# Later blocks of a blocked FFT convolution transformed by residue, with half the matrix products and a second butterfly level on VectorE

## The chip, the cores and the metric

The kernel runs on one core of a Trainium2 chip. TensorE (PE) does matrix products into PSUM, VectorE (DVE) and ScalarE (ACT) do elementwise work, GpSimd (POOL) a little of it, and SyncE (SP) issues most transfers. The metric is the device time of one execution in microseconds (us). Three runs of the kernel before gave 387.19, 388.03 and 388.34 us; the median is 388.03.

## The reference

Two layers of the same two sub-blocks over x of 2048 rows by 512 channels, in bf16. Sub-block A is a gated long convolution, sub-block B a SwiGLU feed-forward network (FFN):

```python
def A(q, k, v, shift_k, ssm_k, ssm_D):          # S = 2048, D = 512
    k_shift = sum(k_pad[:, t:t + S] * shift_k[:, ks - 1 - t] for t in range(4))
    kv = k_shift * v
    y = irfft(rfft(kv, 2 * S) * rfft(ssm_k, 2 * S))[:S]      # along the sequence, per channel
    return q * (y + kv * ssm_D)

def B(x):                                        # F = 1792
    return (silu(x @ w_gate) * (x @ w_up)) @ w_down

x = A_q
x = x + A(layernorm(x), A_k, A_v, ...);  x = x + B(layernorm(x))
x = x + A(layernorm(x), A_k, A_v, ...);  x = x + B(layernorm(x))
```

k, v and the filter do not depend on x, so the convolution result y is the same in both layers and is computed once.

## The kernel before

**Convolution.** The sequence is cut into NB = 4 blocks of L = 512 rows; block b of y is a sum of products of spectra of blocks i and j with i + j = b (an odd-frequency transform of length N = 1024). A block's 512 rows are stored as 128 partitions by R = 4 residues. A spectrum is a tile [128, 4, 2, 512]: four slots of 128 frequencies, a real and an imaginary part, 512 channels. A transform is done partly as products with the constant matrices `fwd` (line 264) and partly as sums and differences on VectorE:

- `spectrum_h(b)` (398): `transpose_h` turns the filter block into rows, `half` (328) makes eight PSUM tiles, two accumulated products of 512 columns each, which ScalarE copies out (`evacuate`, 320); `butterfly` (339) is one level of sums and differences, two VectorE operations of 2048 elements; then `G`, a combination of two blocks' spectra.
- `spectrum_x(b)` (412): `shift_mul` (385) makes the shifted k by 64 small products and multiplies it by v on VectorE, straight out of PSUM (395); then `half` and `butterfly`.
- `product(i, j)` (420): the complex product of X[i] and G[j], 2048 elements to an operation, added into Z[i + j].
- `inverse(k)` (474): two 2048-element operations into `su`, then four PSUM tiles of four accumulated products each, copied out by ScalarE as Y[k].

Block 0 has a path of its own (`direct`, `inverse_direct`).

**FFN.** `ffn` (569) handles a unit: one layer, one block, one half (two of the four residues, 256 rows). In groups of up to four of the 14 tiles of F it makes gate and up products (line 590, by the helper on 252), Silu and copy on ScalarE (593, 597), one multiplication on VectorE (600, tile `ht`), and down products (607) into two PSUM tiles `pd`; at the end VectorE adds these to x (612), and in layer 1 the rows are stored. There are 16 units, in the order block, layer, half. `prologue` (536) comes before a unit: layer norm (`ln_stats`, `normalise`; the reciprocal root on GpSimd, 516), the gating with y (543, 544), the second norm and a transposing transfer of z to `zT`.

**Order.** Nothing is issued where it stands in the text. `add` gives each operation to a `Plan` with an engine, an estimated cost, the buffers that it touches and, for some, a due time; `dues` (99) works due times backwards, and `order` (112) then writes each engine's order out: always the operation that can start first, and among those that can start at about the same time the one with the earliest due time. At run time each engine works its list off in that order. Buffers come from rings of fixed size (228): `pf` 4 and `pc` 2 and `pd` 2 PSUM tiles (FFN, convolution, down products), `s8` 10 spectra, `ht` 5. FFN units get due times from T0 on, DC = 22 us to a unit and DF = 18 in the last block (684). Until T0, idle stretches of PE are filled with dummy products (`dummy`, 179).

**Start.** SP issues k, h, v of block 0, then w_gate, x of block 0, w_up, w_down, x of block 1 (the order that the planner made); ScalarE's queue brings the taps (`tapT`) and D (`dcol`). ScalarE makes `fwd` with a Sin (640) and afterwards runs one Silu ahead of time (643).

Of the kernel before, what the change touches and what calls it, by code (L numbers as in the profile page):

```python
# [9 lines left out]
P = 128  # L10
# [8 lines left out]
NB = 4  # L19
SLK = 5.0  # L20
R = 4

# [23 lines left out]
class Plan:  # L46
# [143 lines left out]
def kernel(  # L190
# [36 lines left out]

    plan = Plan({"h": 1, "k": 1, "v": 1, "hs": 1, "x": 2, "y": 2, "s8": 10, "t4": 2, "n": 2, "z": 3, "zT": 3,
                 "sg": 2, "ht": 5, "st": 8, "mv": 6, "ve": 6, "rs": 6, "pf": 4, "pc": 2, "pd": 2})
# [41 lines left out]

    def load_h(b):
        hn[b] = new("h", "hn", [P, KD, L], parts=1)
        add("SP", 0.55, lambda: nc.sync.dma_start(out=hn[b].t[:], in_=h3[:, :, b * L:(b + 1) * L]), w=[hn[b]], lat=4.5)

    def load_k(b):
        kT[b] = new("k", "kTb", [P, KD, PADL + L], parts=2)
        if b == 0:
            add("POOL", 0.2, lambda: nc.gpsimd.memset(kT[b].t[:, :, 0:PADL], 0.0), w=[(kT[b], (0,))])
            add("SP", 1.5, lambda: nc.sync.dma_start_transpose(out=kT[b].t[:, :, PADL:PADL + L], in_=k3[0:L]),  # L280
                w=[(kT[b], (1,))], lat=3.5)
# [4 lines left out]
    def load_v(b, eng="SP"):  # L286
        vt[b] = new("v", "vt", [P, R, D], parts=R)
        q = nc.sync if eng == "SP" else nc.scalar
        add(eng, 0.6, lambda: q.dma_start(out=vt[b].t[:], in_=v_t[:, b]), w=[vt[b]], lat=4.5)

    def load_x(c):
        xs[c] = new("x", "xc", [P, R, D], parts=R)
        add("SP", 0.7, lambda: nc.sync.dma_start(out=xs[c].t[:], in_=q_t[:, c]), w=[xs[c]], lat=4.5)

    def load_weights(which):
# [4 lines left out]
        add("SP", 0.6, lambda: nc.sync.dma_start(out=wt[which].t[:], in_=src), w=[wt[which]], lat=12.0)  # L300

# [83 lines left out]
    def shift_mul(b, ring, conv):  # L385
        for r in range(R):
            ps = new(ring, "ps", [P, D], F32)

            def go(ps=ps, r=r):
                for dt in range(KD):  # L390
                    mm(ps.t[:, dt * P:(dt + 1) * P],
                       [(kT[b].t[:, dt, PADL + r - j:PADL + r - j + R * (P - 1) + 1:R], dg.t[:, dt, j, :])
                        for j in range(KS)])
            add("PE", pe(KS * KD, P), go, r=[kT[b], dg], w=[ps], conv=conv)
            dve(D, lambda ps=ps, r=r: nc.vector.tensor_tensor(out=vt[b].t[:, r, :], in0=ps.t[:], in1=vt[b].t[:, r, :],  # L395
                                                             op=ALU.mult), [ps], [(vt[b], (r,))], one=True, conv=conv)

    def spectrum_h(b, ring="pc"):
# [7 lines left out]
        h, hp = H[b], H[b - 1]  # L406
        for part, op in ((0, ALU.subtract), (1, ALU.add)):
# [4 lines left out]
    def spectrum_x(b):  # L412
        shift_mul(b, "pc", True)
        ev = spectrum("ev")
        X[b] = spectrum(f"X{b}")
        for par in (0, 1):
            half(vt[b], ev, par, 1.0, "pc", ("ACT", "ACT"), True)
        butterfly(ev, X[b], None, True)

# [54 lines left out]
    def inverse(k):  # L474
        y, z = new_y(k), Z[k]
        su = spectrum("su")
        dve(4 * D, lambda: nc.vector.tensor_add(out=su.t[:, 0:2], in0=z.t[:, 0:2], in1=z.t[:, 2:4]), [z],
            [(su, key((0, 1)))], conv=True)
        dve(4 * D, lambda: nc.vector.tensor_sub(out=su.t[:, 2:4], in0=z.t[:, 0:2], in1=z.t[:, 2:4]), [z],
            [(su, key((2, 3)))], conv=True)  # L480
        for r in range(R):
            ps = new("pc", "ps", [P, D], F32)
            add("PE", pe(4), lambda ps=ps, r=r: mm(ps.t[:], [(iT(f, q), su.t[:, s, part]) for f, q, s, part in INV_TERMS[r]]),
                r=[(su, key((0, 1) if r % 2 == 0 else (2, 3))), inv], w=[ps], conv=True)
            add("ACT", act(D), lambda ps=ps, r=r: nc.scalar.copy(out=y.t[:, r, :], in_=ps.t[:]), r=[ps], w=[(y, (r,))],
# [33 lines left out]

    def normalise(dst, dkeys, view, c, i, o, st):  # L520
        mv, rstd = st
        add("DVE", 0.325, lambda: nc.vector.tensor_scalar(out=view(), in0=xs[c].t[:, i, :], scalar1=mv.t[:, o, 0:1],  # L522
                                                          scalar2=rstd.t[:, o:o + 1], op0=ALU.subtract, op1=ALU.mult),
# [3 lines left out]

    def apply_norm(c, h):
        rows = range(HP * h, HP * h + HP)
        st = ln_stats(c, rows)  # L530
        n = new("n", "n", [P, HP, D], parts=HP)
        for o, i in enumerate(rows):
            normalise(n, (o,), lambda o=o: n.t[:, o, :], c, i, o, st)
        return n

    def prologue(layer, c, h, on_pe=False):
        rows = list(range(HP * h, HP * h + HP))
        sl = slice(rows[0], rows[-1] + 1)
        x, y = xs[c], Y[c]
        n = normed.pop((layer, c, h)) if (layer, c, h) in normed else apply_norm(c, h)  # L540
        zT = zts[layer, c, h] = new("zT", "zT", [P, KD, HP, P], parts=HP)
        if not on_pe:
            dve(HP * D, lambda: nc.vector.tensor_mul(out=n.t[:], in0=n.t[:], in1=y.t[:, sl, :]), [(y, rows)], [n])  # L543
            dve(HP * D, lambda: nc.vector.tensor_add(out=x.t[:, sl, :], in0=x.t[:, sl, :], in1=n.t[:]), [n], [(x, rows)])
            st = ln_stats(c, rows)
            for o, i in enumerate(rows):
                z = new("z", "z", [P, D])
                normalise(z, (0,), lambda z=z: z.t[:], c, i, o, st)
                add("SP", 1.25, lambda z=z, o=o: nc.sync.dma_start_transpose(
# [19 lines left out]
    def ffn(unit, t0, dur):  # L569
# [8 lines left out]
        for fts in groups:  # L578
# [3 lines left out]
            for o in range(0, n, 2):  # L582
# [17 lines left out]
            dve(n * W, lambda sg=sg, ht=ht: nc.vector.tensor_mul(out=ht.t[:], in0=ht.t[:], in1=sg.t[:]), [sg], [ht],  # L600
                due=t0 + k * step)
            for o in range(HP):
                i = HP * h + o

                def go(o=o, fts=fts, ht=ht):
                    for q, ft in enumerate(fts):
                        nc.tensor.matmul(pds[o].t[:], lhsT=ht.t[:, q, o * P:(o + 1) * P], rhs=wt["d"].t[:, ft, :],  # L607
                                         start=(ft == 0), stop=(ft == NF - 1))
                add("PE", pe(n), go, r=[ht, wt["d"]], w=[pds[o]], due=t0 + k * step + 2.0)
        for o in range(HP):  # L610
            i = HP * h + o
            add("DVE", tt1(D), lambda o=o, i=i: nc.vector.tensor_add(out=x.t[:, i, :], in0=x.t[:, i, :], in1=pds[o].t[:]),  # L612
                r=[pds[o]], w=[(x, (i,))], due=t0 + dur + 4)
            if layer == 1:
# [9 lines left out]
    add("POOL", 0.6, lambda: make_identity(nc, ident.t[:]), w=[ident])  # L624
    load_h(0)
    add("ACT", 0.5, lambda: nc.scalar.dma_start(out=tapT.t[:], in_=A_shift_k.rearrange("(dt p) j -> p dt j", p=P)), w=[tapT],
        lat=2.4)
    load_k(0)
    load_v(0)
    add("ACT", 0.5, lambda: nc.scalar.dma_start(out=dcol.t[:], in_=A_ssm_D.rearrange("(dt p o) -> p dt o", p=P, o=1)),  # L630
        w=[dcol], lat=3.0)
    load_x(0)
    ph = new("s8", "ph", [P, NT, P], I32, parts=2)
    for i, (_, r, quarter) in enumerate(BLOCKS):
# [4 lines left out]
        w=[ph])  # L639
    add("ACT", 3.0, lambda: nc.scalar.activation(out=fwd.t[:], in_=ph.t[:], func=ACT.Sin, scale=-math.pi / N, bias=math.pi),  # L640
        r=[ph], w=[fwd])
    warm1 = whole("warm", [P, 1], F32)
    add("ACT", 1.5, lambda: nc.scalar.activation(out=warm1.t[:], in_=nhalf.t[:], func=ACT.Silu), r=[nhalf, fwd], w=[warm1], due=8)
    for dt in range(KD):
# [5 lines left out]
        r=[dcol], w=[hn[0]])  # L650
    load_weights("g")
    hs = transpose_h(0, "pf", (2, 0, 1, 3), False, ("ACT", "DVE"))
# [17 lines left out]
    load_weights("u")  # L670
    load_weights("d")
    load_h(1)
# [10 lines left out]

    T0, DF, DC = 38.0, 18.0, 22.0
    start = {}
# [81 lines left out]
```

## Time and profile before

| | us |
|---|---|
| median of three runs | 388.03 |
| profiled execution | 387.24 |
| its span, first to last instruction | 385.5 |
| PE busy | 369.3 (96%) |
| DVE busy | 282.7 (73%) |
| ACT busy | 189.1 (49%) |
| POOL busy | 35.7 (9%) |

An engine's busy time is the time in which it had at least one instruction under way. Matrix products overlap one another, so PE's busy time is not a measure of its work; the distance from one product's start to the next is. In rows of the timeline the two numbers are start and duration, "x8" is how many instructions were merged into the row, and the bracket at the end tells how long the engine was idle before it and what ended that. In the chain of what ended last the numbers are start and length, counted to the start of the next piece, so that overlap is taken out. In groups the two numbers behind the bar are busy us in all and mean ns of one instruction. In rows by stage, behind each stretch comes its length, and then each engine's busy time with its number of instructions; the PE clock follows as a share of full speed.

### The profile page before, as it was taken

The numbers are of one execution on the slowest core, as the hardware profiler recorded it, in microseconds if no ns is written. First come the engines' busy times: TensorE is split into PE (matmuls) and PEld (weight loads), VectorE is DVE, ScalarE is ACT, GpSimd is POOL, SyncE is SP. The second block draws the span as 40 slices with busy tenths as digits, with TensorE's granted clock in tenths as the row PEclk, the third lists the DMA queues.
The fourth block names the chain that finished last, engine by engine and source line by source line (L and its number), as shares of the span: only waits on it lengthen the run. The fifth ranks groups of instructions, "written<-read, shape, count | busy, mean of one in ns | idle before, by whom it ended". The sixth has DMA issues, their size and how long they took to land.

```text
span 385.5 us, 6975 instructions
## 1 busy us (share of the span) xinstructions
PE 369.3 (96%) x2883; PEld 268.6 (70%) x2926; DVE 282.7 (73%) x504; ACT 189.1 (49%) x320; POOL 35.7 (9%) x42
## 2 busy tenths in 40 slices
PE   8699999999899999999899999999999999999996
PEld 8635776767576776777676677676777777767774
DVE  6388691999998895899999869799963551828212
ACT  4265836344457345544445563564435444444342
POOL 1000100110112000020211000010210100102000
PEclk9989999999999999999999999999999999999999
DMA  8994015110003123101010121001010101010100
GB/s 205 402 311 120 31 24 62 55 27 2 18 19 102 29 53 87 56 5 24 3 27 30 27 57 56 0 2 27 2 27 30 28 30 29 0 29 0 29 27 29
DMA packets 34352, 20.43 MB, mean 53 GB/s; under 512 B 26384, under 2 KB 32272, under 8 KB 34320
## 3 DMA queue, kind: packets, MB, share of 16 engines
q1 hardware_dynamic: 33264, 19.98, 19.7%
q8 instruction: 23, 0.38, 0.4%
q10 hardware_dynamic: 1056, 0.01, 0.2%
q14 instruction: 9, 0.07, 0.1%
HBM read 11.80 MB, written 2.10 MB: 36 GB/s over the span
## 4 chain that ended last, share of the span: by engine, by line
PE 53%; DVE 38%; DMA 3%; POOL 3%; issue 1%; SPq 1%; ACT 1%; DVEq 0%; POOLq 0%
PE pf L252 27%; PE pd L607 14%; PE ps L252 9%; DVE bnst L511 6%; DVE ht L600 4%; DVE t L449 4%; DMA xc<-in_A_q_dram 3%; DVE t L446 3%; POOL rstd L516 3%; DVE xc L612 3%; DVE t L458 2%; DVE n L522 2%; DVE Z L460 2%; PE ps L499 2%; DVE Z L455 1%; DVE n L543 1%
## 5 line engine op out<-in xcount | busy, mean ns | idle before, releaser
L593 ACT ACTIVATE sg<-pf 128x512 bf16<-128x512 f32 x112 | 67.0, 598 | 105.5 <-PE pf L252 102.1
L252 PE MATMUL pf<-zT,wu_sb 128*128 128x256 bf16 x896 | 116.1, 273 | 0.0
L252 PE MATMUL pf<-zT,wg_sb 128*128 128x256 bf16 x896 | 116.1, 273 | 0.0
L607 PE MATMUL pd<-wd_sb,ht 128*128 128x512 bf16 x422 | 102.4, 379 | 6.0 <-DVE ht L600 4.2
L252 PEld LDWEIGHTS <-wg_sb 128*128 128x128 bf16 x896 | 87.3, 98 | 24.2 <-issue 0.2
L252 PEld LDWEIGHTS <-wu_sb 128*128 128x128 bf16 x896 | 87.6, 98 | 12.7
L597 ACT CAST ht<-pf 128x512 bf16<-128x512 f32 x112 | 65.7, 586 | 43.6 <-PE pf L252 43.6
L607 PEld LDWEIGHTS <-ht 128*128 128x128 bf16 x448 | 42.8, 98 | 47.9 <-DVE ht L600 6.8
L600 DVE TENSOR_TENSOR ht<-ht,sg 128x1024 bf16<-128x1024 bf16 x64 | 39.7, 620 | 46.4 <-ACT ht L597 46.4
L516 POOL TENSOR_TENSOR rstd<-ve,nhalf 128x2 f32<-128x2 f32 (+1 forms) x33 | 34.6, 1049 | 319.4 <-DVE ve L514 319.4
L511 DVE BATCH_NORM_STATS2 bnst<-xc 128x6 f32<-128x512 bf16 x64 | 41.3, 684 | 5.1 <-DMA xc<-in_A_q_dram 4.7
L322 ACT ACTIVATE ev<-ps 128x512 bf16<-128x512 f32 x56 | 31.6, 604 | 21.4 <-PE ps L252 14.9
L612 DVE TENSOR_TENSOR xc<-xc,pd 128x512 bf16<-128x512 bf16 x32 | 20.5, 683 | 19.3 <-PE pd L607 19.3
L252 PEld LDWEIGHTS <-fwd 128*128 128x128 bf16 x144 | 14.3, 99 | 17.5 <-issue 6.1
L449 DVE TENSOR_TENSOR t<-X,G 128x2048 bf16<-128x2048 bf16 x18 | 21.9, 1219 | 0.0
L446 DVE TENSOR_TENSOR t<-X,G 128x2048 bf16<-128x2048 bf16 x18 | 21.9, 1218 | 0.0
L252 PE MATMUL ps<-hs,fwd 128*128 128x512 bf16 x58 | 16.7, 401 | 4.2 <-DVE vt L395 4.1
L252 PE MATMUL ps<-vt,fwd 128*128 128x512 bf16 x74 | 19.7, 379 | 0.2
L522 DVE TENSOR_SCALAR n<-xc,mv,rstd 128x512 bf16<-128x512 bf16 x32 | 12.0, 410 | 8.1 <-POOL rstd L516 8.1
L252 PE MATMUL ps<-dg,kTb 128*128 128x128 bf16 x256 | 16.1, 219 | 0.0
L252 PEld LDWEIGHTS <-kTb 128*128 128x128 bf16 x256 | 15.5, 114 | 0.5
L522 DVE TENSOR_SCALAR z<-xc,mv,rstd 128x512 bf16<-128x512 bf16 x32 | 11.8, 409 | 5.0 <-POOL rstd L516 4.9
(59 smaller groups left out, 219.4 us busy)
## 6 DMA issues: line engine op xcount, KB each, us to landing
hn<-in_A_ssm_k_dram SPq DMA_DIRECT2D x4, 512.0 KB, 4.8
vt<-in_A_v_dram SPq DMA_DIRECT2D x4, 512.0 KB, 3.4
xc<-in_A_q_dram SPq DMA_DIRECT2D x4, 512.0 KB, 8.2
out_dram<-xc SPq DMA_DIRECT2D x16, 128.0 KB, 1.7
wg_sb<-in_B_w_gate_dram SPq DMA_DIRECT2D x1, 1792.0 KB, 11.7
wu_sb<-in_B_w_up_dram SPq DMA_DIRECT2D x1, 1792.0 KB, 15.6
wd_sb<-in_B_w_down_dram SPq DMA_DIRECT2D x1, 1792.0 KB, 20.3
zT<-z SPq DMA_TRANSPOSE x30, 2.5
```

The source lines that it names most:

```text
L252: nc.tensor.matmul(o, lhsT=lhsT, rhs=rhs, start=(n == 0), stop=(n == len(terms) - 1))
L322: add("ACT", act(D), lambda: nc.scalar.activation(out=view(), in_=ps.t[:], func=ACT.Copy, scale=scale), r=[ps], w=[(buf, keys)], conv=conv)
L446: dve(n * D, lambda t1=t1, part=part: nc.vector.tensor_mul(out=t1.t[:], in0=x.t[:, sl, 0, :], in1=g.t[:, sl, part, :]), [(x, key(slots, (0 ...
L449: dve(n * D, lambda t2=t2, part=part: nc.vector.tensor_mul(out=t2.t[:], in0=x.t[:, sl, 1, :], in1=g.t[:, sl, 1 - part, :]), [(x, key(slots ...
L511: add("DVE", 0.6, lambda st=st, i=i: nc.vector.bn_stats(out=st.t[:], in_=xs[c].t[:, i, :]), r=[(xs[c], (i,))], w=[st])
L516: add("POOL", 0.75, lambda: nc.gpsimd.tensor_tensor(out=rstd.t[:], in0=ve.t[:], in1=nhalf.t[:].to_broadcast((P, n)), op=ALU.pow), r=[ve, n ...
L522: add("DVE", 0.325, lambda: nc.vector.tensor_scalar(out=view(), in0=xs[c].t[:, i, :], scalar1=mv.t[:, o, 0:1], scalar2=rstd.t[:, o:o + 1], ...
L593: add("ACT", act(D), lambda ps=ps, o=o, sg=sg: nc.scalar.activation(out=sg.t[:, o:o + 2, :], in_=ps.t[:], func=ACT.Silu), r=[ps], w=[(sg, ...
L597: add("ACT", act(D), lambda ps=ps, o=o, ht=ht: nc.scalar.copy(out=ht.t[:, o:o + 2, :], in_=ps.t[:]), r=[ps], w=[(ht, (o // 2,))], due=t0 + ...
L600: dve(n * W, lambda sg=sg, ht=ht: nc.vector.tensor_mul(out=ht.t[:], in0=ht.t[:], in1=sg.t[:]), [sg], [ht], due=t0 + k * step)
L607: nc.tensor.matmul(pds[o].t[:], lhsT=ht.t[:, q, o * P:(o + 1) * P], rhs=wt["d"].t[:, ft, :], start=(ft == 0), stop=(ft == NF - 1))
L612: add("DVE", tt1(D), lambda o=o, i=i: nc.vector.tensor_add(out=x.t[:, i, :], in0=x.t[:, i, :], in1=pds[o].t[:]), r=[pds[o]], w=[(x, (i,))] ...
```

## The change

- **Transforms by residue.** For h and x of blocks 1 to 3, `by_residue` makes eight PSUM tiles with one product each, instead of two; `forward4` then does two butterfly levels on VectorE: `fold2` (two operations of 2048 elements), `sum_diff` (two of 1024) and `rotated` (four of 512). `inverse` does the same two levels first and then two products for each of its four PSUM tiles, instead of four.
- **PSUM read by ScalarE.** The shifted k of blocks 1 to 3 is copied out of PSUM by ScalarE (`KV_ACT`), and VectorE multiplies from SBUF. The FFN's output tiles are copied out by ScalarE (`PD_ACT`), and VectorE adds 1024 elements at a time from SBUF. The other switches (`ST_ACT`, `Z_ACT`, `N_ACT`) are off, and the functions behind them are not used.
- **Loads.** h of block 0 goes on ScalarE's queue ahead of taps and D; on SP, k, v and x of block 0 come ahead of the three weights. The one early Silu comes before the Sin.
- **Planner.** T0 is 34 instead of 38; the due times of the `ht` multiplications and of the FFN's end are 3 us earlier (`HSL`); fewer dummy products for a given idle time.

```diff
+PD_ACT, KV_ACT, ST_ACT = True, True, False
+HSL = 3.0
+Z_ACT, N_ACT = False, False
...
-                    n = int((b - a - 0.2) / 0.062)
+                    n = int((b - a - 0.4) / 0.085)
...
     def shift_mul(b, ring, conv):
...
+            if KV_ACT and b:
+                ks = new("ks", "ks", [P, D])
+                add("ACT", act(D), lambda ps=ps, ks=ks: nc.scalar.copy(out=ks.t[:], in_=ps.t[:]), r=[ps], w=[ks], conv=conv)
+                dve(D, lambda ks=ks, r=r: nc.vector.tensor_mul(out=vt[b].t[:, r, :], in0=ks.t[:], in1=vt[b].t[:, r, :]),
+                    [ks], [(vt[b], (r,))], conv=conv)
+                continue
...
+    def by_residue(rows, ev, scale, ring, engs, conv):
+        for r in range(R):
+            for part, f in enumerate(("C", "nS")):
+                ps = new(ring, "ps", [P, D], F32)
+                add("PE", pe(1), lambda ps=ps, f=f, r=r: mm(ps.t[:], [(fT(f, r), rows.t[:, r, :])]),
+                    r=[(rows, (r,)), fwd], w=[ps], conv=conv)
+                evacuate(ps, ev, (2 * r + part,), lambda r=r, part=part: ev.t[:, r, part], scale,
+                         engs[(2 * r + part) % len(engs)], conv)
+    def fold2(src, dst, conv):
+        for lo, op in ((0, ALU.add), (2, ALU.subtract)):
+            dve(4 * D, lambda lo=lo, op=op: nc.vector.tensor_tensor(out=dst.t[:, lo:lo + 2], in0=src.t[:, 0:2],
+                                                                    in1=src.t[:, 2:4], op=op),
+                [src], [(dst, key((lo, lo + 1)))], conv=conv)
+    def sum_diff(m, i, j, dst, k, l, conv):
+        for slot, op in ((k, ALU.add), (l, ALU.subtract)):
+            dve(2 * D, lambda slot=slot, op=op: nc.vector.tensor_tensor(out=dst.t[:, slot], in0=m.t[:, i], in1=m.t[:, j],
+                                                                        op=op),
...
+    def rotated(m, i, j, dst, plus, minus, conv):
+        for slot, part, op in ((plus, 0, ALU.subtract), (plus, 1, ALU.add), (minus, 0, ALU.add), (minus, 1, ALU.subtract)):
+            dve(D, lambda slot=slot, part=part, op=op: nc.vector.tensor_tensor(
+                out=dst.t[:, slot, part], in0=m.t[:, i, part], in1=m.t[:, j, 1 - part], op=op),
...
+    def forward4(rows, name, scale, ring, conv):
+        ev = spectrum(name)
+        by_residue(rows, ev, scale, ring, ("ACT",), conv)
+        m = spectrum("m")
+        fold2(ev, m, conv)
+        sum_diff(m, 0, 1, ev, 0, 2, conv)
+        rotated(m, 2, 3, ev, 3, 1, conv)
+        return ev
     def spectrum_h(b, ring="pc"):
         hs = transpose_h(b, ring, (0, 2), True)
-        ev = spectrum("ev")
-        H[b] = spectrum("H")
-        for par in (0, 1):
-            half(hs, ev, par, 2.0 / N, ring, ("ACT", "ACT"), True)
-        butterfly(ev, H[b], None, True)
+        h, hp = forward4(hs, "H", 2.0 / N, ring, True), H[b - 1]
+        H[b] = h
...
     def inverse(k):
         y, z = new_y(k), Z[k]
-        su = spectrum("su")
...
+        m = spectrum("m")
+        fold2(z, m, True)
+        sum_diff(m, 0, 1, z, 0, 2, True)
+        rotated(m, 2, 3, z, 1, 3, True)
         for r in range(R):
             ps = new("pc", "ps", [P, D], F32)
-            add("PE", pe(4), ...
+            add("PE", pe(2), lambda ps=ps, r=r: mm(ps.t[:], [(iT("C", r), z.t[:, r, 0]), (iT("nS", r), z.t[:, r, 1])]),
...
     def ffn(unit, t0, dur):
...
             dve(n * W, lambda sg=sg, ht=ht: nc.vector.tensor_mul(out=ht.t[:], in0=ht.t[:], in1=sg.t[:]), [sg], [ht],
-                due=t0 + k * step)
+                due=t0 + k * step - HSL)
...
+        if PD_ACT:
+            dn = new("dn", "dn", [P, HP, D], parts=HP)
+            for o in range(HP):
+                add("ACT", act(D), lambda o=o: nc.scalar.copy(out=dn.t[:, o, :], in_=pds[o].t[:]), r=[pds[o]], w=[(dn, (o,))],
+                    due=t0 + dur + 3 - HSL)
+            dve(HP * D, lambda: nc.vector.tensor_add(out=x.t[:, sl, :], in0=x.t[:, sl, :], in1=dn.t[:]), [dn], [(x, rows)],
+                due=t0 + dur + 4 - HSL)
...
-    load_h(0)
+    load_h(0, "ACT", -60)
     add("ACT", 0.5, lambda: nc.scalar.dma_start(out=tapT.t[:], ...
-    load_k(0)
-    load_v(0)
+    load_k(0, -60)
+    load_v(0, -59)
...
-    load_x(0)
+    load_x(0, -58)
+    load_weights("g", -57)
+    load_weights("u", -56)
+    load_weights("d", -55)
...
-    T0, DF, DC = 38.0, 18.0, 22.0
+    T0, DF, DC = 34.0, 18.0, 22.0
```

More of the change, by code (lines that the diff above doesn't have):

```diff
@@ L413, in spectrum_x @@
         shift_mul(b, "pc", True)
[L414 to L418, printed above, removed]
+        X[b] = forward4(vt[b], f"X{b}", 1.0, "pc", True)
     def product(i, j, slots=range(4), conv=True):
@@ new lines, in shift_of, with normalise @@
+    def shift_of(st, n):
+        mv, rstd = st
+        nmr = new("ve", "nmr", [P, n], F32)
+        add("DVE", 0.08, lambda: nc.vector.scalar_tensor_tensor(out=nmr.t[:], in0=mv.t[:, :, 0], scalar=-1.0, in1=rstd.t[:],
+                                                                op0=ALU.mult, op1=ALU.mult), r=[mv, rstd], w=[nmr])
+        return nmr
+    def normalise(dst, dkeys, view, c, i, o, st, nmr=None):
+        mv, rstd = st
+        if nmr is not None:
+            add("ACT", act(D), lambda: nc.scalar.activation(out=view(), in_=xs[c].t[:, i, :], func=ACT.Identity,
+                                                            scale=rstd.t[:, o:o + 1], bias=nmr.t[:, o:o + 1]),
+                r=[(xs[c], (i,)), nmr, rstd], w=[(dst, dkeys)])
+            return
@@ L639 @@
         w=[ph])
-    add("ACT", 3.0, lambda: nc.scalar.activation(out=fwd.t[:], in_=ph.t[:], func=ACT.Sin, scale=-math.pi / N, bias=math.pi),
+    warm1 = whole("warm", [P, 1], F32)
+    add("ACT", 1.5, lambda: nc.scalar.activation(out=warm1.t[:], in_=nhalf.t[:], func=ACT.Silu), r=[nhalf], w=[warm1], due=-50)
+    add("ACT", 1.8, lambda: nc.scalar.activation(out=fwd.t[:], in_=ph.t[:], func=ACT.Sin, scale=-math.pi / N, bias=math.pi),
         r=[ph], w=[fwd])
-    warm1 = whole("warm", [P, 1], F32)
-    add("ACT", 1.5, lambda: nc.scalar.activation(out=warm1.t[:], in_=nhalf.t[:], func=ACT.Silu), r=[nhalf, fwd], w=[warm1], due=8)
     for dt in range(KD):
```

84 lines of the change are left out of this document (52 added, 32 removed).

## The prediction

> **What bounds the kernel now.** I read the head of the page, then the busy time of the engines by stage, then the waits, then the chain that ended last. The profiled execution took 387.24 us, 1.7 us over its span and 0.8 us under the median of 388.03.
>
> ```profile
> span 385.5 us, 6975 instructions
> PE 369.3 (96%) x2883; PEld 268.6 (70%) x2926; DVE 282.7 (73%) x504; ACT 189.1 (49%) x320; POOL 35.7 (9%) x42
> ```
>
> I cut the span at the first FFN product (43.15), the end of block 3's inverse butterflies (281.80), the first FFN product of block 3 (308.70) and the last product:
>
> ```profile
> core 0: us, PE busy (x) PEld busy (x) DVE busy (x) ACT busy (x) POOL busy (x), PEclk, DMA share, GB/s
> 0.00:43.15 43.15, 37.17 (x329) 24.91 (x333) 28.60 (x73) 23.94 (x38) 3.61 (x13) 0.96 0.78 238
> 43.15:281.80 238.65, 232.74 (x1817) 170.34 (x1844) 208.94 (x334) 118.98 (x205) 24.54 (x21) 1.00 0.14 32
> 281.80:308.70 26.90, 26.69 (x197) 19.49 (x200) 12.92 (x32) 13.01 (x22) 2.69 (x3) 1.00 0.13 30
> 308.70:381.80 73.10, 72.66 (x545) 53.82 (x550) 31.38 (x66) 33.13 (x56) 4.89 (x5) 1.00 0.08 19
> 381.80:385.50 3.70, 0.00 (x0) 0.00 (x0) 0.87 (x2) 0.00 (x0) 0.00 (x0) 0.93 0.21 71
> ```
>
> Four stages with different limits. PE's busy time overlaps itself, so I count its work by steps between starts, from the chain:
>
> ```profile
> 56.90 1.75 PE pf L252 x16
> 58.64 0.86 PE ps L252 x4
> 59.51 1.73 PE pd L607 x8
> 70.67 1.20 DVE xc L612 x2
> 132.94 2.27 DVE G L408 x2
> 229.76 0.89 PE ps L252 x16
> ```
>
> An FFN unit is 112 gate/up products (12.2 us) and 28 down products (6.1): 18.3, and four of them are the 73.1 us of the last stage, where PE alone is the bound. From 43.15 to 381.80 there are 16 units (292.5), 128 transform products of 0.216 (27.6), 192 shift products at 0.89/16 (10.7) and some 3 us of transposes and remainders: 333.8 of 338.65. PE waits for under 5 us, most of it here:
>
> ```profile
> DVE ht L600 <- ACT ht L597: 18.7, 8, 6.2
> DVE n L522 <- POOL rstd L516: 6.1, 9, 0.9
> PE pd L607 <- DVE ht L600: 4.2, 6, 1.3
> ```
>
> (waits between 43.15 and 308.70). But from 43 to 282 DVE is close behind: 208.94 of 238.65, idle 29.7. The two limits lie within a few per cent of each other, and the change shortens one and lengthens the other.
>
> **The change, part by part.**
>
> *PE.* Six later spectra (h and x of blocks 1 to 3) go from 16 products of 512 columns to 8, three inverses likewise: 72 x 0.216 = 15.6 us less. Eight of these (h of block 1) lie in the start-up; 64 x 0.216 = 13.8 lie after it. All of them are on PE's queue, which is nearly full, so they count whole as long as DVE keeps up.
>
> *DVE.* Durations and steps of its operations:
>
> ```profile
> L347 DVE TENSOR_TENSOR X<-ev 128x2048 bf16<-128x2048 bf16 x3 | 3.7, 1221 | 0.1
> L395 DVE TENSOR_TENSOR vt<-ps,vt 128x512 bf16<-128x512 f32 x16 | 10.7, 682 | 0.0
> L435 DVE TENSOR_TENSOR t<-X,G 128x1024 bf16<-128x1024 bf16 x8 | 5.3, 687 | 0.0
> L439 DVE TENSOR_TENSOR Z<-t,t 128x512 bf16<-128x512 bf16 x8 | 3.0, 420 | 0.0
> L612 DVE TENSOR_TENSOR xc<-xc,pd 128x512 bf16<-128x512 bf16 x32 | 20.5, 683 | 19.3 <-PE pd L607 19.3
> ```
>
> (groups: us in all and mean ns of one behind the bar) and, from the order of time, pairs of them back to back:
>
> ```profile
> 31.40 1.29 DVE L435 TENSOR_TENSOR t<-X,G 128x1024 bf16<-128x1024 bf16 x2
> 32.60 0.76 DVE L439 TENSOR_TENSOR Z<-t,t 128x512 bf16<-128x512 bf16 x2
> ```
>
> Back to back, a 2048 takes 2.27/2 = 1.135; a pair of 1024s spans 1.29, one of them 0.69, so the step is 0.60; a 512 in SBUF 0.76 - 0.42 = 0.34; a 512 out of PSUM 1.20/2 = 0.60. A transform had two 2048s (2.27). It gets two 2048s, two 1024s and four 512s: 2.27 + 1.20 + 1.36 = 4.83, or 2.56 more; nine transforms make 23.0. The shifted k, through ScalarE for blocks 1 to 3, saves 12 x (0.60 - 0.34) = 3.1. The FFN output: one 1024 out of SBUF for two 512s out of PSUM, 0.6 saved in each unit; ten of the twelve units before block 3 have theirs before 281.8: 6.0. Net in that stretch +13.9, to 222.9 us.
>
> A rule of the Trainium skill speaks against many small operations: VectorE: DVE Perf Modes, "The DRAIN you can't avoid", says that the next operation starts when the pipe of the one before has emptied, and its rules ask for few operations. The same page's section on two instructions with no wait lets an unheld one start earlier, which is what the trace shows (2.27 for two of 1.22). With whole durations the transforms would cost 9 x 3.05 = 27.5 and the net would be about +17.6.
>
> *ScalarE.* 32 + 12 copies more, at the 0.59 of its others:
>
> ```profile
> L597 ACT CAST ht<-pf 128x512 bf16<-128x512 f32 x112 | 65.7, 586 | 43.6 <-PE pf L252 43.6
> L322 ACT ACTIVATE ev<-ps 128x512 bf16<-128x512 f32 x56 | 31.6, 604 | 21.4 <-PE ps L252 14.9
> ```
>
> 26 us on an engine busy half the time (118.98 of 238.65): nothing, hidden by its idle time. Evictions per transform stay at eight, but each now follows one product (0.216) instead of two, so two conv buffers at 0.6 per eviction hold PE unless FFN products stand between. In the middle there are FFN products to interleave; if not, 72 x (0.3 - 0.216) = 6 us at most; I take 0. The wait of the shifted k for a copy adds about 0.8 us of latency per residue, hidden by the queue of products; in return both buffers come free without DVE. The down buffers too: PE's next unit no longer waits for DVE's add. Taking 3 us off the due time of the ht products moves them ahead of transform work on DVE; it answers the 4.2 us that PE waits for ht, and may save none to all of that. I count none, since DVE gets fuller.
>
> *Start-up.* The loads:
>
> ```profile
> 1.73 8.53 PE L733 MATMUL wm<-ident 128*128 128x128 bf16 x113 [1.73 <-POOL ident masks.py:199]
> 3.58 0.43 SPq L300 DMA_DIRECT2D wg_sb<-in_B_w_gate_dram  x1
> 4.05 1.40 SPq L293 DMA_DIRECT2D xc<-in_A_q_dram  x1
> 8.21 0.18 DVE L649 TENSOR_TENSOR hn<-hn,dcol 128x4 bf16<-128x4 bf16 x1 [0.57 <-DMA hn<-in_A_ssm_k_dram]
> 10.32 1.05 PE L374 MATMUL pt<-ident,hn 128*128 128x128 bf16 x16
> 16.57 1.29 DVE L511 BATCH_NORM_STATS2 bnst<-xc 128x6 f32<-128x512 bf16 x2 [4.73 <-DMA xc<-in_A_q_dram]
> 24.98 7.07 PE L252 MATMUL ps<-vt,fwd 128*128 128x512 bf16 x32
> 33.88 1.09 DVE L439 TENSOR_TENSOR Z<-t,t 128x512 bf16<-128x512 bf16 x3
> ```
>
> x of block 0 is issued behind the gate weights and lands at 16.5; DVE stands at its statistics with the four shift products queued behind, and PE behind these. Now h, k, v, x (2.1 MB) go ahead of all weights. The next late things: h, on ScalarE's queue and about 1.5 us earlier; the taps and D now behind h on that queue (bounds 0 to +2 us for both, from h's own 8.2); and fewer warm-up products, which now hold PE until 10.3 though h is there at 8.4. At the 0 to 43 stage's 238 GB/s, 2.1 MB land at about 9. Shift products then run from 10 to 13.6, their products with v end at 14.3, the block-0 h spectrum is eviction-paced (8 x 0.6) to 18.5, X0 begins 6.5 us earlier than 24.98. DVE from 9.5 has about 18 to 20 us of work (statistics, norms, butterflies, products), so the last Z ends at 29.5, not 34.97: the gain is 5 (bounds 1 if h, taps and D come late, 7 if all of x's delay comes off). First FFN product: 38.2. A Silu table loaded before the Sin may have to be loaded once more, between nothing and one load:
>
> ```profile
> L643 ACT ACT_TABLE_LOAD x1 | 1.3, 1283 | 0.0
> ```
>
> ScalarE has time for it before the first FFN eviction: 0.
>
> *End.* DVE's two adds:
>
> ```profile
> 381.38 1.28 DVE L612 TENSOR_TENSOR xc<-xc,pd 128x512 bf16<-128x512 bf16 x2 [1.12 <-PE pd L607]
> ```
>
> become copy, copy, one add: 0.59 + 0.69 and a hand-over behind the last product, against 1.28. +0.4 (0 to +1).
>
> **The sum.** Block 3's FFN can start on PE's account at 38.2 + 265.55 - 4.7 - 13.8 = 285.2. On DVE's account its inverse butterflies must be done, and then comes latency, of which today's trace shows (the last row in us from issue to landing):
>
> ```profile
> 280.63 1.22 DVE L479 TENSOR_TENSOR su<-Z 128x2048 bf16<-128x2048 bf16 x1
> 296.32 0.69 DVE L543 TENSOR_TENSOR n<-n,Yk 128x1024 bf16<-128x1024 bf16 x1 [4.51 <-ACT Yk L485]
> 300.66 0.74 DVE L522 TENSOR_SCALAR z<-xc,mv,rstd 128x512 bf16<-128x512 bf16 x2
> ```
>
> ```profile
> zT<-z SPq DMA_TRANSPOSE x30, 2.5
> ```
>
> The butterflies end at 281.8; the inverse products and copies that follow are in no hurry today and need about 3 (four copies of 0.59 behind the first product); then 5.1 from 296.3 to z at 301.4, 2.5 for the transposing DMA, and 0.9 of hand-overs: 11.5. DVE's idle time in the stretch is the unknown: not under 6 (the waits for rstd stay), not over today's 29.7. Most of today's is waiting for ht while the next spectrum is still on PE; that production halves, so I take 18, the middle. 38.2 + 222.9 + 18 + 11.5 = 290.6: DVE sets it, and PE waits for 5 us, about as much as now. Then 73.1 of pure FFN, 363.7; tail 4.1, span 367.8; 369.5 as an execution, 370.3 as a median.
>
> **Rivals.**
> - *PE stays the only bound* (DVE's waits shrink to those for rstd, start-up gains 7): 36.2 + 247.0 + 73.1 + 4.1 + 2.5 = 363. For it: PE now waits only 4.2 us; against: DVE would run at over 95%.
> - *DVE's idle time stays at 29.7*, since it comes from the order of FFN work and not from missing spectra: 302.3 at block 3, 382. For it: eight waits for ht, 18.7 us; against: they fall where spectra are being made.
> - *Small dependent operations cost their whole duration* (the rule above): +3.7 us on DVE, 374. The quoted pairs speak against it.
> - *No change*: idle as now and a start-up gain of 1 or less, about 386 to 388. What speaks against it is x's delay, plainly on the chain.
> - *Slower*: ht products queue behind a transform operation in DVE's in-order queue, and PE waits at every down group. Today 6 of 48 groups before block 3 wait, 0.7 each. At 48 x 0.7 = 33.6: 38.2 + 247.0 + 33.6 + 73.1 + 4.1 + 2.5 = 398.5. It decides from about 23 us of such waits, 33 groups. Against it: ht is put forward by 3 us and PE has other units' products to run.
>
> **How the numbers follow.** Forecast (365 to 376) 0.54; whole durations 0.05; PE alone 0.12; idle stays (376 to 386) 0.20; no change 0.04; slower 0.05. 0.3% is 1.2 us, about what can be told from no change. Faster: 0.91, same 0.04, slower 0.05. The range runs from PE alone, 363, to just short of idle stays, 381.
>
> **What would show it.** First FFN product near 38 with x's statistics starting near 10; PE's transform products 72 fewer and no new PE wait on evictions; DVE at about 92% from there to block 3's inverse, with the waits for ht fallen by half; block 3 starting near 290 and 73 us of FFN behind it. Wrong if: h, taps or D land late and the start-up gains nothing; PE's waits for ht multiply; or single products wait on two conv buffers.

## The result and the profile after

The changed kernel takes 374.66 us (median; 374.59 to 374.82), against 387.83 of the kernel before beside it: ratio 0.9662, interval 0.9645 to 0.9679, 13.2 us faster. The forecast was 370.3 in a range of 363 to 381. The profiled execution took 374.7, its span is 372.8. All medians here are of fast runs: one execution of e7 took 465.63 us at a granted clock of 0.754 and is left out.

The head of its page, and the busy time by stage. The first two cuts are the same events as before: the first FFN product (38.52) and the end of block 3's inverse butterflies (275.30). The third is 295, by when block 3's FFN has just begun (294.03), and the last is 369, just behind the last product. In the kernel before, block 3's first gate product was at 305.95 (224 of them, four units, are left from there on); the cut at 308.70 is only the point that lies 73.1 us ahead of the last product's end.

```profile
span 372.8 us, 6865 instructions
PE 354.1 (95%) x2814; PEld 258.9 (69%) x2814; DVE 292.8 (79%) x542; ACT 209.0 (56%) x363; POOL 36.2 (10%) x42
```

```profile
core 0: us, PE busy (x) PEld busy (x) DVE busy (x) ACT busy (x) POOL busy (x), PEclk, DMA share, GB/s
0.00:38.52 38.52, 34.16 (x302) 22.77 (x303) 30.18 (x75) 23.82 (x39) 3.60 (x13) 1.00 0.86 267
38.52:275.30 236.78, 227.15 (x1811) 167.27 (x1810) 223.76 (x383) 135.98 (x241) 27.56 (x22) 1.00 0.14 33
275.30:295.00 19.70, 19.70 (x151) 14.59 (x150) 9.79 (x25) 10.86 (x19) 1.61 (x3) 1.00 0.11 27
295.00:369.00 74.00, 73.14 (x557) 54.22 (x555) 28.49 (x62) 38.37 (x66) 3.44 (x5) 1.00 0.11 19
```

VectorE now works 223.76 of 236.78 us (94.5%) where it worked 208.94 of 238.65 (87.5%). PE's waits in the whole run (us in total, times, longest; the two largest that are not in the start-up):

```profile
PE pd L685 <- DVE ht L678: 8.1, 10, 1.2
PE pf L255 <- DMA zT<-z: 1.4, 1, 1.4
```

Before, the first of these was 4.2 us in 6 waits. (`ht` is the product of gate and up that the down products need, `zT` the transposed input of a unit.) What such a wait looks like, from the timeline of VectorE and of PE:

```profile
77.12 0.74 DVE L598 TENSOR_SCALAR z<-xc,mv,rstd 128x512 bf16<-128x512 bf16 x2 [0.58 <-POOL rstd L555]
77.77 0.69 DVE L678 TENSOR_TENSOR ht<-ht,sg 128x1024 bf16<-128x1024 bf16 x1
78.37 1.22 DVE L489 TENSOR_TENSOR t<-X,G 128x2048 bf16<-128x2048 bf16 x1
79.62 1.22 DVE L498 TENSOR_TENSOR t<-t,t 128x2048 bf16<-128x2048 bf16 x1
80.76 0.42 DVE L678 TENSOR_TENSOR ht<-ht,sg 128x512 bf16<-128x512 bf16 x1
```

```profile
78.51 1.90 PE L685 MATMUL pd<-wd_sb,ht 128*128 128x512 bf16 x8 [1.17 <-DVE ht L678]
81.24 1.04 PE L685 MATMUL pd<-wd_sb,ht 128*128 128x512 bf16 x4 [0.83 <-DVE ht L678]
```

Two operations of 2048 elements stand in VectorE's queue between two ht products; PE has issued all the gate and up products that are ahead in its own list, and waits.

The start-up and the end, in order of time:

```profile
6.69 2.50 DVE L736 TENSOR_TENSOR dg<-ident,tapT 128x512 bf16<-128x512 bf16 x4 [1.47 <-DMA tapT<-in_A_shift_k_dram]
6.90 11.59 SPq L296 DMA_DIRECT2D xc<-in_A_q_dram  x1
9.74 0.69 DVE L550 BATCH_NORM_STATS2 bnst<-xc 128x6 f32<-128x512 bf16 x1 [0.47 <-DMA xc<-in_A_q_dram]
27.44 1.09 DVE L479 TENSOR_TENSOR Z<-t,t 128x512 bf16<-128x512 bf16 x3
28.07 0.64 PE L377 MATMUL pt<-ident,hn 128*128 128x128 bf16 x8 [1.17 <-DMA hn<-in_A_ssm_k_dram]
38.52 1.04 PE L255 MATMUL pf<-zT,wg_sb 128*128 128x256 bf16 x8
365.38 2.75 PE L685 MATMUL pd<-wd_sb,ht 128*128 128x512 bf16 x12
367.74 1.07 ACT L692 CAST dn<-pd 128x512 bf16<-128x512 f32 x2 [1.57 <-PE pd L685]
368.85 0.69 DVE L695 TENSOR_TENSOR xc<-xc,dn 128x1024 bf16<-128x1024 bf16 x1 [2.22 <-ACT dn L692]
```

The statistics of x start at 9.74 instead of 16.57; the last Z ends at 28.5 instead of 35.0; the first FFN product comes at 38.52 instead of 43.15. Between Z and that product lie 10.0 us, against 8.2 before: h of block 1 is late, issued behind the transfer that held SP's queue from 6.90 to 18.5.

### The profile page after: what moved, and what is told of

Its sections match the earlier page's. It is cut to its first block, busy times and chain, and to the rows that moved or that the text cites. A ratio compares the mean times of both kernels' runs of the same rounds, so it can differ in the third digit from the quotient of the medians.

```text
span 372.8 us, 6865 instructions
## 1 busy us (share of the span) xinstructions
PE 354.1 (95%) x2814; PEld 258.9 (69%) x2814; DVE 292.8 (79%) x542; ACT 209.0 (56%) x363; POOL 36.2 (10%) x42
## 4 chain that ended last, share of the span: by engine, by line
DVE 45%; PE 41%; DMA 4%; POOL 3%; ACT 3%; issue 1%; SPq 1%; ACTq 0%; POOLq 0%
PE pf L255 24%; PE pd L685 12%; DVE bnst L550 6%; DVE m L420 5%; DVE ht L678 5%; PE ps L255 4%; POOL rstd L555 3%; DVE t L486 3%; DVE t L489 3%; DMA hn<-in_A_ssm_k_dram 3%; DVE t L498 2%; DVE Z L500 2%; DVE Z L495 2%; DVE n L598 2%; DVE z L598 2%; DVE xc L695 1%
## 5 line engine op out<-in xcount | busy, mean ns | idle before, releaser
L685 PE MATMUL pd<-wd_sb,ht 128*128 128x512 bf16 x448 | 106.6, 379 | 8.1 <-DVE ht L678 8.1
L692 ACT CAST dn<-pd 128x512 bf16<-128x512 f32 x32 | 17.6, 591 | 23.0 <-PE pd L685 23.0
L489 DVE TENSOR_TENSOR t<-X,G 128x2048 bf16<-128x2048 bf16 x18 | 21.9, 1217 | 0.0
L486 DVE TENSOR_TENSOR t<-X,G 128x2048 bf16<-128x2048 bf16 x18 | 21.9, 1216 | 0.0
L325 ACT ACTIVATE X<-ps 128x512 bf16<-128x512 f32 x32 | 18.5, 599 | 5.5 <-PE ps L255 5.4
L695 DVE TENSOR_TENSOR xc<-xc,dn 128x1024 bf16<-128x1024 bf16 x16 | 11.0, 687 | 10.6 <-ACT dn L692 10.5
L255 PEld LDWEIGHTS <-fwd 128*128 128x128 bf16 x96 | 9.3, 98 | 8.8 <-issue 0.4
L255 PE MATMUL ps<-vt,fwd 128*128 128x512 bf16 x56 | 15.2, 379 | 0.1
```

The source lines that it names most:

```text
L255: nc.tensor.matmul(o, lhsT=lhsT, rhs=rhs, start=(n == 0), stop=(n == len(terms) - 1))
L325: add("ACT", act(D), lambda: nc.scalar.activation(out=view(), in_=ps.t[:], func=ACT.Copy, scale=scale), r=[ps], w=[(buf, keys)], conv=conv)
L486: dve(n * D, lambda t1=t1, part=part: nc.vector.tensor_mul(out=t1.t[:], in0=x.t[:, sl, 0, :], in1=g.t[:, sl, part, :]), [(x, key(slots, (0 ...
L489: dve(n * D, lambda t2=t2, part=part: nc.vector.tensor_mul(out=t2.t[:], in0=x.t[:, sl, 1, :], in1=g.t[:, sl, 1 - part, :]), [(x, key(slots ...
```

## The experiments

Theory A: the time is the sum of one list, PE's: its start, its products, its waits; VectorE's load enters only through the waits. Theory B: VectorE's load from 38 to 275 sets the time, and PE's saved products are worth nothing by themselves. A's sum by itself proves little, since whatever delays PE is booked in it as a wait; what tells the two apart is how many waits a load on VectorE brings. Ratios are to the kernel before, run beside each.

**One part, or all but one.**

```diff
 e1: after, with the old half/butterfly transforms and
-PD_ACT, KV_ACT, ST_ACT = True, True, False
+PD_ACT, KV_ACT, ST_ACT = False, False, False
-HSL = 3.0
+HSL = 0.0
```


> The changed kernel with the old transforms, the old FFN output and shifted k on VectorE and the old due times: of the change only the loads, the early Silu, the dummy products and T0 remain. Theory A (the time is PE's start + PE's work + PE's waits for ht, and VectorE's load sets only the waits): the first FFN product comes at about 40 (the h spectrum of block 1 has its 16 products again), PE's work is the old 333.8, waits about 4: 40 + 333.8 + 4 + 4.1 + 2.5 = 384, 3 to 4 us under before. Theory B (VectorE's load sets the time, PE's products are worth nothing of themselves): its load is the old one, so the same 383 to 384 by the earlier start alone. This run sizes the start-up; it does not tell A from B.

```diff
 e2: before, with spectrum_h, spectrum_x and inverse of after
-            half(hs, ev, par, 2.0 / N, ring, ("ACT", "ACT"), True)
-        butterfly(ev, H[b], None, True)
+        h, hp = forward4(hs, "H", 2.0 / N, ring, True), H[b - 1]
```


> The kernel before with the transforms by residue alone (spectra of blocks 1 to 3 and inverses), all else as before. A: start at 42 to 43, PE's work 320, and VectorE, with 23 us more and none of the relief, makes PE wait some 12 us: 42.5 + 320 + 12 + 4.1 + 2.5 = 381 (378 to 384). B: VectorE needs 208.9 + 23 = 232 with its old idle time of 29.7 between the start and block 3's inverse: 43 + 232 + 29.7 + 11.5 + 73.1 + 4.1 + 2.5 = 396, slower than before.

```diff
 e3: after, with
-PD_ACT, KV_ACT, ST_ACT = True, True, False
+PD_ACT, KV_ACT, ST_ACT = False, False, False
```


> The changed kernel with the FFN output and the shifted k read from PSUM by VectorE again. VectorE gets 9.1 us more up to block 3's inverse. A: PE's waits for ht grow from 8 to some 12 to 15 us, and the tail is 0.5 to 0.9 shorter: 378 to 381. B: the whole 9.1 comes on top: 384.

```diff
 e5: after, with spectrum_h, spectrum_x and inverse of before
-        h, hp = forward4(hs, "H", 2.0 / N, ring, True), H[b - 1]
+            half(hs, ev, par, 2.0 / N, ring, ("ACT", "ACT"), True)
+        butterfly(ev, H[b], None, True)
```


> The changed kernel with the old transforms (16 products and one butterfly level). PE gets 15.6 us more, VectorE 23 less. A: first FFN product near 40, PE's work 333.8, PE's waits for ht 2 to 4 instead of 9.5: 40 + 333.8 + 3 + 5.1 + 2 = 384. B: VectorE's load is what counts and falls by 23: faster than the changed kernel, 360 to 372.

| | us | ratio, interval |
|---|---|---|
| e1, start-up alone | 382.57 | 0.9870 (0.9842 to 0.9898) |
| e2, transforms alone | 384.89 | 0.9932 (0.9911 to 0.9953) |
| e3, all but the copies by ScalarE | 379.68 | 0.9793 (0.9764 to 0.9822) |
| e5, all but the transforms | 382.87 | 0.9877 (0.9844 to 0.9910) |
| after | 374.66 | 0.9662 (0.9645 to 0.9679) |

B falls: e5 takes 21.9 us off VectorE (270.9 us busy against 292.8) and is 8.2 us slower than after, and e2 is 0.7% faster than before, not 396. A holds with its waits. In e5 PE waited 3.3 us for ht and 1.0 for an inverse's sums, in after 8.1 for ht and 1.4 for zT: of the 13.8 us of products saved behind the start, 5 to 6 came back as waits and 8.2 are left.

The parts do not add singly. ScalarE's copies are worth 5.0 us beside the new transforms (e3 to after). Beside the old ones e5 is 0.3 slower than e1; that step has the copies and the earlier due times in it together, so neither was sized there alone. That the copies pay only where VectorE is full is what these two steps suggest. e1 beat its sum of 384 by 1.4: its first FFN product came at 38.37, not 40, so the start-up gives 5.4 us by itself, and the eight products of block 1's h that the new transforms save there are hidden.

Two numbers did not come about as expected. e2 missed A's 378 to 384: PE's waits for ht were 12.5 us, as expected, but the start came at 44.28, not 42 to 43 (its trace is of the slowest of its ten runs, 386.54). e3 lies within A's 378 to 381, but not by A's way: its waits for ht were 7.2 us, not 12 to 15. Waits for zT (3.3) and for VectorE to empty PSUM tiles of the shifted k (2.4) came instead, 12.9 behind the start against 9.5 in after, and the clock fell.

e2 and e3 show something more: the granted clock (the share of TensorE's full speed that the profile reports). Rows of e2 by stretches of 4 us, and its PE timeline:

```profile
80.00:84.00 4.00, 1.93 (x18) 1.47 (x16) 3.93 (x7) 1.17 (x2) 0.00 (x0) 1.00 0.00 0
84.00:88.00 4.00, 2.50 (x7) 0.77 (x8) 3.97 (x9) 0.60 (x1) 0.99 (x1) 0.80 0.01 2
88.00:92.00 4.00, 1.90 (x5) 0.74 (x6) 3.97 (x6) 0.00 (x0) 0.00 (x0) 0.50 0.32 64
92.00:96.00 4.00, 4.00 (x25) 2.43 (x24) 2.72 (x4) 1.18 (x2) 0.00 (x0) 0.84 0.00 0
```

```profile
85.32 2.55 PE L637 MATMUL pd<-wd_sb,ht 128*128 128x512 bf16 x7 [3.39 <-DVE ht L630]
90.10 3.44 PE L637 MATMUL pd<-wd_sb,ht 128*128 128x512 bf16 x8 [2.23 <-DVE ht L630]
```

After a wait of 3.4 us the clock is halved; eight down products then take 3.44 us instead of 1.90. By those shares (0.20 + 0.50 + 0.16) x 4 = 3.4 us of clock are lost beside the wait itself, though part of that falls into the next wait. e3 has a dip at the same place:

```profile
81.81 2.30 PE L685 MATMUL pd<-wd_sb,ht 128*128 128x512 bf16 x7 [4.51 <-DVE ht L678]
```

with 0.84 and 0.73 granted in the two stretches from 80 to 88, and a second one, 0.57 from 260 to 264, behind a wait of 2.1 us for zT: 1.7 us of clock each. Of e3's 5.0 us the waits are 3.4 and the clock up to 3.4, while its tail is 1.0 shorter. In after, with no wait over 1.4 behind the start, the clock is 1.00 from 38.52 to 369.

**The order on VectorE.**

```diff
 e4                      e10
-HSL = 3.0              -HSL = 3.0
+HSL = 0.0              +HSL = 6.0
```


> The changed kernel with the due times of the ht products and of the FFN's end put back (HSL 0). Theory A (VectorE is nearly full, and PE's 8.1 us of waiting for ht come from ht products standing behind transform work in VectorE's queue): PE's waits for ht grow by 1 to 4 us, 376 to 378.5. Rival C (the waits come from VectorE's load and not from the order in its queue, since the planner puts first whatever can start first and the due time only breaks ties): no change, 374 to 375.5.

> The changed kernel with the ht products and the FFN's end due 6 us earlier than in the old plan instead of 3. If the waits for ht come from the order in VectorE's queue alone, more of them go: waits for ht 8.1 to 4 to 6 us, 371 to 373. If VectorE is simply full by then, the transforms come later instead, the waits move to the start of a block or stay: 374 to 377.

e4: 376.78, ratio 0.9717 (0.9698 to 0.9737): 2.1 us slower than after. The number is A's, but not by A's way, so it is a hit by luck: PE's waits for ht did not grow, they came to 7.2 us. One of them was 2.88 long, and the clock fell behind it:

```profile
81.10 3.10 PE L685 MATMUL pd<-wd_sb,ht 128*128 128x512 bf16 x8 [2.88 <-DVE ht L678]
```

```profile
80.00:84.00 4.00, 2.90 (x9) 1.08 (x10) 4.00 (x6) 0.00 (x0) 0.00 (x0) 0.71 0.16 33
84.00:88.00 4.00, 4.00 (x29) 3.00 (x28) 2.75 (x5) 2.13 (x4) 0.00 (x0) 0.87 0.00 0
```

(0.29 + 0.13) x 4 = 1.7 us. One of e4's four runs had a mean clock of 0.999, the others 0.995, and took 375.56 against 376.77 to 376.83. So some 1.2 of the 2.1 us seem to go with the dip, and 0.9 stay; there is no trace of that run, so why they stay is open.

e10: 375.05, 0.9666 (0.9646 to 0.9686), no gain over after in the median: waits for ht 8.1 us again, in 6 pieces, one of 2.7 with a clock of 0.58 behind it (1.7 us). Here too one run of four was without the dip by its mean clock (1.000, the others 0.993 to 0.995), and it took 373.78, 0.9 less than after. So the due times did not change how long PE waits for ht in all (7.2, 8.1, 8.1 us for 0, 3 and 6). They changed how the waits are cut up, and the setting of 3 is the one of these whose trace has no wait long enough for a dip. Whether 6 would be better with its longest wait broken up was not run.

**Relief for VectorE from ScalarE.**

```diff
 e6_z_act                                e6_zn_act
-Z_ACT, N_ACT = False, False            -Z_ACT, N_ACT = False, False
+Z_ACT, N_ACT = True, False             +Z_ACT, N_ACT = True, True
```


> The changed kernel with the second norm's scaling (z) moved from VectorE to ScalarE in all but the first prologue (the switch Z_ACT): per prologue two 512-element operations (0.65 to 0.74 us) leave VectorE and one small one (about 0.1 to 0.2) comes; 15 prologues, some 7 us off VectorE in all, 6 of it before block 3. Theory A: PE's waits for ht fall from 8.1 by some 2 to 4 us: 371 to 373. Rival D (the relief is eaten by latency: z now waits for a small VectorE operation after the root and for ScalarE's queue, so zT comes later and PE waits for it at the start of units): 375 to 378, with waits for zT over 3 us.

> As with z on ScalarE, and the first norm's scaling (n) of blocks 1 to 3 too: some 12 us off VectorE in all, 10 of it before block 3; ScalarE gets 54 operations of 0.6 (32 us). Theory A: 369.5 to 372, waits for ht below 4. Rival D: 375 to 380, waits for zT or for PSUM tiles that ScalarE empties late.

e6_z_act: 376.89, 0.9727 (0.9710 to 0.9743); e6_zn_act: 378.88, 0.9780 (0.9735 to 0.9825), the median of two runs near 377.3 (mean clock 0.998) and two near 380.5 (0.990). Both kernels are slower than after in every run. Waits of e6_z_act, and the group:

```profile
ACT z L594 <- DVE nmr L587: 18.7, 10, 3.4
PE pd L685 <- DVE ht L678: 5.8, 9, 1.2
PE ps L255 <- ACT X L325: 2.3, 3, 1.4
```

```profile
L594 ACT ACTIVATE z<-xc,nmr,rstd 128x512 bf16<-128x512 bf16 x30 | 23.2, 813 | 18.7 <-DVE nmr L587 18.7
```

VectorE's busy time fell from 292.8 to 284.6 and 278.1 us, and PE's waits for ht with it, from 8.1 to 5.8 and 4.8: the part of A that says that waits for ht come with VectorE's load fits. But new waits took the gain: all of PE's waits behind the start came to 10.0 and 11.0 us, against 9.5 in after. ScalarE stood 18.7 us before its z operations, with evictions queued behind, and PE waited for PSUM (2.3 us). That is D's number by another wait than D named for e6_z_act: zT cost PE 1.2 us there, not over 3. In e6_zn_act PE did wait 3.5 us once for zT, and the clock was 0.50 in the 4 us behind it. In e6_z_act two waits of 0.7 and 1.4 us lay within 3.2 us, and the clock was 0.71 from 132 to 136 and 0.86 from 136 to 140: 1.7 us. Its profiled execution (378.23, the slowest of four; the others took 376.75 to 376.98) is 3.7 us longer in span than that of after; start (+0.3), clock (+1.7), PSUM (+2.3) and ht (-2.3) make 2.0 of it, and the rest stays open.

**The loads, and the end.**

```diff
 e7 and e9: h and k of block 1 ahead of w_down and x of block 1
-    load_weights("d", -55)
...
     load_h(1)
+    load_weights("d", -55, [hn[1]])          # w_down waits for h of block 1
...
-        load_x(c)
+        load_x(c, None, [kT[1]] if c == 1 else [])   # x of block 1 waits for k of block 1
 e7 also:
-    load_h(0, "ACT", -60)
+    load_h(0, "ACT", -57)          # behind the taps and D
 e8:
-        if PD_ACT:
+        last = unit == (1, NB - 1, HP - 1)
+        if PD_ACT and not last:
...
-            if not PD_ACT:
+            if not PD_ACT or last:
```


> The changed kernel with two orders of loads mended: taps and D ahead of h of block 0 on ScalarE's queue, and h and k of block 1 ahead of w_down and of x of block 1 on SP's (in the changed kernel h of block 1 was issued behind a transfer that held SP's queue for 11.6 us, and PE waited for it at 28.1). Theory A: PE's 1.2 us wait at 28 and its 0.4 us wait for the D term at 9.3 go; the first FFN product comes at 36.8 to 37.8 instead of 38.5, and all of it comes through, since PE is the queue that counts: 373 to 374. Rival E (VectorE sets the pace from 40 on, so an earlier first product is waited away later): 374.5.

> The changed kernel with h of block 0 first on ScalarE's queue as there, and only SP's order mended: h and k of block 1 ahead of w_down and of x of block 1. Each engine's order of operations stays that of the changed kernel. Theory A (an earlier start comes through whole, since PE's list is nearly without gaps afterwards): h lands at 8.2 again, PE's 1.2 us wait at 28.1 goes, the first FFN product comes at 37.0 to 37.6, and the end 1.0 to 1.5 earlier: 373.2 to 373.7. Rival E (VectorE sets the pace from 40 on): 374.5.

> The changed kernel with the last unit's FFN output added straight from PSUM by VectorE, as before the change, one row group at a time. The tail (from the last products' end to the end of the span) is 5.1 us in the changed kernel and was 4.1: it falls by 0.4 to 1.0, and nothing else moves: 373.7 to 374.3.

e7: 375.56 (median of three), 0.9690 (0.9669 to 0.9711), a miss. The taps and D ahead of h held h up:

```profile
10.73 1.35 PE L377 MATMUL pt<-ident,hn 128*128 128x128 bf16 x16 [2.96 <-DMA hn<-in_A_ssm_k_dram]
```

against 8.51 in after. From issue to landing h took 8.9 us here and 3.5 in after, where it was there long before PE used it, right behind the warm-up products (1.73 + 6.73 = 8.46); the 8.2 at which e9's expectation lets h land is about that first use, and not the landing. Behind the wait of 3.0 the clock was 0.94 and 0.63 in the two stretches from 8 to 16, 1.7 us. The wait for h of block 1 was gone all the same, and the first FFN product came at 39.77. With h first again, e9: 373.49, 0.9635 (0.9619 to 0.9652), first FFN product

```profile
37.27 1.04 PE L255 MATMUL pf<-zT,wg_sb 128*128 128x256 bf16 x8
```

1.25 us earlier than in after, and the end 1.2 earlier, with each engine's order of operations kept; PE's waits for ht were 8.5 us in 10 pieces, in after 8.1 in 10. e7 and e9 move the start by +1.25 and -1.25, and the spans (374.0 and 371.5 against 372.8) follow by +1.2 and -1.3: the start comes through whole. This does not tell A from E, though, since VectorE's list moves with it: the first butterfly of block 1's h starts at 35.39 in e9, 36.64 in after and 37.89 in e7. e8: 374.00, 0.9645 (0.9629 to 0.9662); the adds stand at

```profile
368.20 1.28 DVE L701 TENSOR_TENSOR xc<-xc,pd 128x512 bf16<-128x512 bf16 x2 [1.12 <-PE pd L685]
```

and the span ends 3.8 us behind the last product's end (368.59), not 4.7: 0.7 off the median. (By the rows the tail was 4.7 in after and 3.7 before, 0.4 less than the expectation has for each.)

**Both together**, e11.

```diff
 e11: after, with the edits of e9 and of e8
```


> The changed kernel with both mended: SP's order (h and k of block 1 ahead of w_down and x of block 1) and the last unit's output added straight from PSUM. Under theory A the start and the tail are separate terms of one sum on PE's list and add: 1.2 + 0.7 less than the changed kernel, 372.6 to 373.0. If VectorE sets the pace in between, the earlier start is lost again and only the tail remains: 374.0.

372.63 us (372.12 to 374.20), 0.9616 (0.9596 to 0.9635): 2.0 less than after, about the sum of the two (1.2 + 0.7), and the fastest of all kernels here. One of its five runs, with a mean clock of 0.995 against 0.998 to 1.000, is the 374.20.

## Why the prediction was right, and where it was off

- *What bounds it: half right.* PE's work is as predicted: 38.52 + 320.0 + 9.5 (waits) = 368.0, and the last product ends at 365.38 + 2.75 = 368.13. But the forecast's sum let VectorE's account set the start of block 3 (290.6: "DVE sets it"). In the trace block 3's first product follows the ones ahead of it on PE's list without a wait, so PE's list set it. On the way there PE and VectorE take turns. In the chain of what ended last, the share of VectorE has passed that of PE (shares of the span, before, then after):

```profile
PE 53%; DVE 38%; DMA 3%; POOL 3%; issue 1%; SPq 1%; ACT 1%; DVEq 0%; POOLq 0%
DVE 45%; PE 41%; DMA 4%; POOL 3%; ACT 3%; issue 1%; SPq 1%; ACTq 0%; POOLq 0%
```

- *Start-up: right in size, 38.2 against 38.52, in part by luck.* x was the late transfer (9 predicted, 9.74). The last Z came 1 us earlier than predicted (28.5, not 29.5), and the way from there to the first FFN product was 1.3 longer (10.0, not 8.7). Of the next-late things the taps were bounded (1.47 us of waiting); h of block 1 was not named, and cost 1.2 us, which e9 took back. One thing I missed: in the kernel before, PE's idle stretch before its first spectrum had cost clock too. The quoted row of the first stage shows 0.96, that is 1.7 us, and the same stage now 1.00. How much of the gain is that stays open, since e1 has a dip as large between 8 and 16 and its first FFN product still came at 38.37.
- *VectorE's load: right.* 222.9 us predicted up to block 3's inverse, 223.76 measured; a transform's second level costs what the pairs said (chain of after: steps to the next piece):

```profile
36.64 2.37 DVE m L420 x2
39.04 1.29 DVE H L426 x2
40.33 1.34 DVE H L433 x4
```

5.0 us against 4.83; the four small ones take 0.335 each. The rival of whole durations (0.42 each) is out. It had been taken from the Trainium skill's page VectorE: DVE Perf Modes, "The DRAIN you can't avoid"; the same section says that a next operation that is not held starts earlier, and the trace agrees with that (0.335 from start to start).
- *The step that was mis-sized: PE's waits, 5 us predicted, 9.5 measured.* I had taken two accounts, PE's and VectorE's, each to the start of block 3, and let the later one win. VectorE's idle time came out at 13.0, not 18 (its own waits for ht were 18.7 us before and are 5.5 from 38.52 to 294.03). Its butterflies were done at 275.3, not 279.1, and by that account block 3 could have started at 286.8. It started at 294.0, because PE had waited 9.5 us for ht and zT on the way, in units of blocks 0 to 2, and PE's list has no slack to make them up. Two queues that are each nearly full delay each other all along, not only at the end of a stretch. The slower rival had the right mechanism, with a third of the waiting it needed (8.1 of 23 us). That the total came as near as it did has luck in it: with 13.0 in place of 18 the forecast's own sum gives 365.3, so the idle time that it took too long stood in for the waits that it took too short.
- *The due times: wrong.* I counted them at nothing; they are worth 2.1 us (e4), some 1.2 of it clock by that kernel's one run without the dip.
- *The tail: 0.4 predicted.* It is 4.7 us from the last product's end instead of 3.7; e8 gives 0.7 back.
- *ScalarE's copies: right* that they hide; the relief they bring is worth 5.0 us (e3), part of it clock. Two conv buffers did not hold PE in the middle. The Silu table was not loaded again: the trace of after has one table load, ahead of the early Silu, where that of before has two.

The sum of the misses: start +0.3, waits and remainders +4.1 (1.0 of it in the last stage, which took 74.1 us and not 73.1), tail +0.6, 5.0 us in the span (372.8 against 367.8).

## What to carry to other kernels

When work is moved from a nearly full engine to one that is about to become full, count both engines' lists, and add a price for the waits of each on the other in every stretch where both are nearly full. Here VectorE went from 87.5% to 94.5% of such a stretch, PE's waits for it went from 4.2 to 8.1 us, and 40% of the saved matrix time went that way. Relief for the second engine was worth 5.0 us beside the new transforms, and together with the earlier due times nothing beside the old ones. It must not put a new wait into the queue of the engine that helps. Look at the longest single wait of the matrix engine too, and not at the sum of its waits alone. In a start-up, look for the transfer that is late next, and at what is queued ahead of it.

## What the runs showed of the hardware that I had not expected

A wait of PE costs more than its length once it is long enough. Behind single waits of 2.7 (e10), 2.9 (e4), 3.4 (e2), 3.5 (e6_zn_act) and 4.5 us (e3), and in the start-up of 3.0 (e7) and 3.4 (the kernel before), the granted clock fell, to 0.50 in the worst stretches of 4 us, and was back at 1.00 within 4 to 12 us. Added up over the stretches, the loss was 1.7 us each time, and 3.4 in e6_zn_act and over the two waits of e2. Behind the waits of after, up to 1.4 us, the clock stayed at 1.00. In between it went either way: a single wait of 2.1 left it at 1.00 in e10 and brought it to 0.57 in e3, and it fell where PE stood twice close together, for 0.7 and 1.4 us in e6_z_act and for 0.5 and 1.3 in the start-up of e1. The Trainium skill (TensorE: Matmul & The Clock Gate, "Why this matters for your kernels") asks for no idle gaps of more than about 3 us between bursts; these runs agree in kind, with 2.7 us enough once and 2.1 us enough once and not enough once.

A transfer of 512 KB (h of block 0) issued behind two transfers of 4 KB and 1 KB (taps and D) on the same queue landed 8.9 us after its issue in e7, and 3.5 and 3.6 us after it in after and e9, where it went ahead of them. What in the two small transfers holds it up was not separated.
